# Gated outer-product attention and a leaky-ReLU MLP: from (chunk, batch) units to quads of four batches, with a new instruction order

## The chip, the cores and the metric

The kernel runs on one core of one Trainium2 chip. The metric is device time of one execution in microseconds (us), lower is better. The time before is 181.54 us, the median of three runs (181.17 to 182.75).

The engines of the core are named as in the profile: PE (matrix multiply, with PEld for its weight loads), ACT (scalar engine), DVE (vector engine), POOL (GpSimd) and SP, whose queue only issues DMAs here. Each engine works through its own list of instructions in order and waits at an instruction until what that instruction needs is there.

## The reference

There are 4 batches, 8 heads, 768 tokens, 48 elements per head. Per head a 48 x 48 state is decayed by a gate and gets an outer product at each token; the result y is laid out as 3072 tokens x 384 and goes through two matrix multiplies with a leaky ReLU between them.

```
f = 1.0 / (1.0 + np.exp(-f_logit))
for t in range(S):
    state = f[:, :, t, :, None] * state + np.einsum('bhd,bhe->bhde', k[:, :, t], v[:, :, t])
    y[:, :, t] = np.einsum('bhd,bhde->bhe', q[:, :, t], state)
...
h = x @ w_in                     # 3072 x 384  @  384 x 2048
g = np.maximum(0.01 * h, h)
return g @ w_out                 # 3072 x 2048 @ 2048 x 384
```

Inputs and output are float32; the matrix multiplies take bf16.

## The kernel before

**Tiling.** The sequence is cut into 6 chunks of 128 tokens. A unit `u` is one chunk of one batch, `u = 4 * chunk + batch`, so there are 24 units; a pair `m` is two neighbouring units. Inside a unit the recurrence is turned into matrix multiplies: cumulated log gates give two decay factors `em` and `a`; k is multiplied by `em` and q by `a`; both are turned so that the head's elements lie on the partitions; scores k x q are masked to the upper triangle; `mix` adds (state x q) and (scores x v); the state takes k x v and is scaled by the decay at the chunk's end (`a_end`).

**Chunk 0** (units 0 to 3) is already worked as one block of four batches, 4 neighbouring tokens per partition (functions with the prefix `q_`). The change leaves its arithmetic as it is.

**Chunks 1 to 5, before.** Each unit has tokens on the partitions. Its steps, with lines of the profile:

- `load_part` (L169): f, k, q and v of a unit, one DMA each on SP's queue, 128 tokens x 8 heads x 48 floats; each contiguous piece in memory is 48 floats, 192 bytes. There are 80 such loads.
- `gate_exp` (L339) and `gate_ln` (L342) on ACT; `gate_pe` (L348, L351): one 384-column matmul with the triangle `ut`, and four 1-column matmuls for the chunk's end; `decay_em` (L355), `decay_a` (L358, L360) on ACT, reading the matmul's bank.
- `k_scale` (L370) and `q_scale` (L374) on DVE or POOL; `cast_v` (L145).
- Turning k and q: by PE for units 4 to 9 (`turn_pe` L383, then `turn_k`, `turn_q`), by a DMA transpose for each pair from unit 10 on (`turn2_dma` L393).
- `score_pe` (L420; L428 for single units), `mask` (L431, DVE), `mix_pe` (L438 state part, L441 score part), `y_out`, `state_pe` (L449), `state_dve` (L457, L458), `state_pool` (L463, L332).
- Turning y: by PE (`x_pe` L472, `x_out`) for units 0 to 17, by DMA transposes (`x2_dma` L397) for pairs 9 to 11.
- `up` (L482): for one pair, a group `g` of two 128-wide slices of w_in, 3 matmuls of 256 columns each; `up_act` (L487, ACT) applies the leaky ReLU to a whole bank of 512 columns. Pair 2 goes as two single units (`up1`, L493, 128 columns).
- `down` (L502): a half is 8 matmuls of 384 columns for one unit; `put` copies the result out of PSUM and `out_dma` (L526) writes 128 rows. The last unit is cut into two column halves (`down_cols` L507, `put_cols`, `out_cols` L517).

**Order.** Nothing is scheduled by a compiler. After `manual_schedule()` a list of some 850 calls, written out one per line, gives the order of every engine's instructions and of SP's DMAs; the last argument of a call is the PSUM bank (0 to 7) that it uses. PE, ACT, DVE, POOL and SP each take their part of that list in that order. The weights come by DMAs on POOL's queue (`load_w_in` L185, two pieces; `load_w_out` L190, four pieces), placed in the list among chunk 0's steps. `idle_pe` (L137) puts matmuls on zeros into the early part.

## Time and profile before

| What | Value |
|---|---|
| time, median of 3 runs | 181.54 us (181.17 to 182.75) |
| profiled execution, span from first to last instruction | 180.2 us |
| granted PE clock | 0.998 |
| instructions | 4849 |
| DVE, ACT, POOL busy | 92.0, 124.4, 57.9 us |
| moved by DMA | 31.31 MB in 109398 packets, 100800 of them under 512 bytes |

The profile gives the span of the profiled execution and no time of its own beside it; the median of the runs is 1.3 us above the span, and that difference is what lies around the first and last instruction and between one execution and another. "Busy" for PE is from a matmul's start to its modelled end, and neighbouring matmuls overlap, so the time that a matmul costs is read from the distance between starts in the chain of waits, not from its own duration. The same holds for ACT and DVE, where an instruction begins before the one ahead of it has quite ended.

### The profile page before, as it was taken

To read this page: it belongs to the slowest core of one execution; us is meant where nothing else is said; L and a number is where in the kernel's file an instruction comes from. 1 tells how busy PE (TensorE), PEld (TensorE's weight loads), DVE (VectorE), ACT (ScalarE), POOL (GpSimd) and SP (SyncE) were. 2 spreads that over 40 slices of the span, in tenths; PEclk is the share of its full clock that TensorE was granted. 3 is DMA by queue.
4 is the path that set the end of the run, shared out by engine and by line. 5 is a ranking of instruction groups with operands and counts; after the bars stand their busy time and mean duration, and the time that the engine had idled before them with its cause. 6 is when DMAs were issued, how large, how long until landed. Compare 5 with 4: busy or idle time off the path is not lost.

```text
span 180.2 us, 4849 instructions
## 1 busy us (share of the span) xinstructions
PE 171.4 (95%) x1919; PEld 137.8 (76%) x1919; DVE 92.0 (51%) x211; ACT 124.4 (69%) x264; POOL 57.9 (32%) x107
## 2 busy tenths in 40 slices
PE   7689999999999999899999999999999999999992
PEld 5365899677878897597789687789876697798672
DVE  7779860287888735335376186696543266000000
ACT  2779999286887789767488776668795562596331
POOL 7077570023256444700446052634072100000000
PEclk9999999999999999999999999999999999999999
DMA  5999999899997989999699899999999982720112
GB/s 154 312 299 162 197 208 214 156 201 190 155 205 125 215 172 224 165 216 208 147 239 251 181 183 185 209 213 173 203 155 209 224 237 48 60 77 0 44 48 86
DMA packets 109398, 31.31 MB, mean 174 GB/s; under 512 B 100800, under 2 KB 108096, under 8 KB 109376
## 3 DMA queue, kind: packets, MB, share of 16 engines
q1 hardware_dynamic: 107440, 27.47, 79.5%
q0 software_dynamic: 1376, 3.15, 9.5%
q10 hardware_dynamic: 560, 0.39, 0.7%
q8 instruction: 15, 0.25, 0.7%
q14 instruction: 7, 0.06, 0.1%
HBM read 25.17 MB, written 4.72 MB: 166 GB/s over the span
## 4 chain that ended last, share of the span: by engine, by line
PE 58%; SPq 25%; DMA 11%; issue 1%; ACT 1%; DVE 1%; DVEq 0%
SPq L169 24%; PE ps L482 24%; PE ps L502 23%; DMA v_raw<-in_v_dram 6%; DMA f_raw<-in_f_logit_dram 3%; PE ps L420 2%; DMA fq<-in_f_logit_dram 2%; PE ps L441 2%; PE ps L507 1%; PE ps L438 1%; PE ps L348 1%; SPq L74 1%; PE ps L472 1%; PE ps L449 1%; DVE v_b L145 1%
## 5 line engine op out<-in xcount | busy, mean ns | idle before, releaser
L502 PE MATMUL ps<-w_out_b,gT 128*128 128x384 bf16 x368 | 65.9, 326 | 0.0
L487 ACT ACTIVATE gT<-ps 128x512 bf16<-128x512 f32 x88 | 51.5, 602 | 19.1 <-PE ps L482 16.7
L482 PE MATMUL ps<-xT,w_in 128*128 128x256 bf16 x528 | 63.3, 273 | 1.0 <-DVE xT L145 1.0
L482 PEld LDWEIGHTS <-w_in 128*128 128x128 bf16 x528 | 56.4, 114 | 3.0 <-issue 1.2
L502 PEld LDWEIGHTS <-gT 128*128 128x128 bf16 x368 | 34.6, 98 | 19.8
L431 DVE TENSOR_TENSOR wm<-ps,ut 128x512 bf16<-128x512 f32 x40 | 24.9, 683 | 14.5 <-ACT gT L487 4.9
L370 POOL TENSOR_TENSOR kqh<-k_raw,em_t 128x384 bf16<-128x384 f32 x12 | 11.4, 951 | 33.3 <-ACT em_t L355 28.1
L143 ACT COPY osb<-ps 128x384 f32<-128x384 f32 (+1 forms) x22 | 10.2, 465 | 17.0 <-PE ps L502 15.2
L332 POOL CAST sb<-sf 64x192 bf16<-64x192 f32 x40 | 14.5, 363 | 14.9 <-PE ps L438 12.8
L145 DVE CAST v_b<-v_raw 128x384 bf16<-128x384 f32 x14 | 7.1, 505 | 16.0 <-DMA v_raw<-in_v_dram 15.9
L374 DVE TENSOR_TENSOR kqh<-q_raw,a_t 128x384 bf16<-128x384 f32 x13 | 10.0, 770 | 8.0 <-DMA q_raw<-in_q_dram 7.3
L339 ACT ACTIVATE f_raw<-f_raw 128x384 f32<-128x384 f32 x20 | 10.6, 532 | 4.8 <-DMA f_raw<-in_f_logit_dram 4.6
L342 ACT ACTIVATE lf<-f_raw 128x384 bf16<-128x384 f32 x20 | 10.5, 527 | 0.4
L358 ACT ACTIVATE a_t<-ps 128x384 bf16<-128x384 f32 x20 | 9.8, 494 | 1.1 <-PE ps L351 0.9
L145 DVE CAST xn<-ps 128x384 bf16<-128x384 f32 x15 | 8.2, 556 | 4.1 <-PE ps L441 3.4
L355 ACT ACTIVATE em_t<-ps 128x384 bf16<-128x384 f32 x20 | 9.9, 501 | 0.2 <-PE ps L351 0.2
L463 POOL TENSOR_TENSOR sf<-sf,a_end 128x192 f32<-128x192 f32 x16 | 9.5, 592 | 0.4
L145 POOL CAST v_b<-v_raw 128x384 bf16<-128x384 f32 x6 | 3.1, 510 | 19.8 <-DMA v_raw<-in_v_dram 19.8
L137 PE MATMUL ps<-fill 128*128 128x256 bf16 x37 | 7.3, 353 | 1.4 <-DVE fill L102 1.3
L374 POOL TENSOR_TENSOR kqh<-q_raw,a_t 128x384 bf16<-128x384 f32 x7 | 7.0, 1003 | 4.2 <-issue 2.6
L370 DVE TENSOR_TENSOR kqh<-k_raw,em_t 128x384 bf16<-128x384 f32 x8 | 5.9, 752 | 3.7 <-ACT em_t L355 3.7
L441 PE MATMUL ps<-v_b,wm 128*128 128x48 bf16 x160 | 7.2, 183 | 0.0
(89 smaller groups left out, 201.8 us busy)
## 6 DMA issues: line engine op xcount, KB each, us to landing
out_dram<-osb SPq DMA_DIRECT2D x23, 192.0 KB, 3.4
f_raw<-in_f_logit_dram SPq DMA_DIRECT2D x20, 192.0 KB, 4.6
k_raw<-in_k_dram SPq DMA_DIRECT2D x20, 192.0 KB, 4.6
q_raw<-in_q_dram SPq DMA_DIRECT2D x20, 192.0 KB, 4.5
v_raw<-in_v_dram SPq DMA_DIRECT2D x20, 192.0 KB, 4.2
w_in<-in_moe_w_in_dram POOLq DMA_DIRECT2D x2, 768.0 KB, 9.8
w_out_b<-in_moe_w_out_dram POOLq DMA_DIRECT2D x4, 384.0 KB, 8.4
kq<-in_k_dram SPq DMA_DIRECT2D x1, 768.0 KB, 6.6
```

Source lines behind the costliest of these rows:

```text
L145: eng.tensor_copy(out=out, in_=in_)
L169: eng.dma_start(out=t, in_=src[b, :, c * C:(c + 1) * C, :].rearrange("h t d -> t h d"))
L332: nc.gpsimd.tensor_copy(out=state_b[b][r, :, e * D:(e + 1) * D], in_=state_f[b][r])
L339: nc.scalar.activation(raw[u]["f"], raw[u]["f"], AF.Exp, scale=-1.0)
L342: nc.scalar.activation(lfs[u % R_LF][:, :, 0:D], raw[u]["f"], AF.Ln, bias=1.0)
L370: eng.tensor_mul(khs[u % R_KQS][:, :, 0:D], raw[u]["k"], em_ts[u % R_EM])
L374: eng.tensor_mul(qhs[u % R_KQS][:, :, 0:D], r["q"], a_ts[u % R_EM])
L431: nc.vector.tensor_mul(wms[e][u % R_WM], bank(bk).rearrange("p (i n) -> p i n", i=P2), ut[:, None, :].to_broadcast([128, P2, 128]))
L441: nc.tensor.matmul(bank(bk)[:, h * D:(h + 1) * D], wms[h % 2][u % R_WM][:, h // 2, :], v_b[:, h, :], start=False, stop=(h == H - 1))
L482: nc.tensor.matmul(bank(bk)[:, i * 256:(i + 1) * 256].rearrange("p (a n) -> p a n", a=2), w_in_p[ff // 8][:, kk, ff // 4 % 2, :, ff % 4], ...
L487: nc.scalar.activation(gTs[m % GBUFS][:, 2 * g:2 * g + 2].rearrange("p f a n -> p (f a n)"), bank(bk), AF.Prelu, alpha=0.01)
L502: nc.tensor.matmul(bank(bk)[:, 0:KD], g_part(u)[:, ff, :], w_out_b[:, ff, :], start=(ff == 0), stop=(ff == NF - 1))
```

## The change

From chunk 1 on the unit of work for gates, loads, turning and `up` is a quad: one chunk of all four batches, laid out as chunk 0 already is. Partition `4t + b` holds 4 neighbouring tokens `4t .. 4t+3` of batch `b`.

- **Loads.** One f, one k and one q load for a chunk (`load_all`, contiguous pieces of 768 bytes, 768 KB), with two buffers each. v goes in four loads of 32 partitions (`load_v`), still in pieces of 192 bytes.
- **Gates.** ACT takes exp and ln on half the heads at a time, 128 x 768. Three additions on DVE or POOL (`g_sum`) cumulate within a partition, `g_cast` makes bf16 of the last, one 384-column matmul (`g_pe`) with a new matrix `before` sums over the partitions ahead of the same batch, four 4-column matmuls with `same` give the chunk's end, and `g_add` (DVE, 128 x 768, reading PSUM) adds that to all four tokens. `g_em` and `g_a` are the exponentials.
- **Scaling.** `g_k` and `g_q` write `khQ` and `qhQ`, each in four parts by pairs of heads, two on DVE and two on POOL as a rule.
- **Turning.** Chunks 1 and 2 by PE (`t_pe`, four groups of 8 transposes, `t_out`), chunks 3 to 5 by four DMA transposes each (`t_dma`). A copy `kh_dma` (four DMAs from SBUF to SBUF for chunks 1 to 4) brings k back to one batch per tile for `state_pe`.
- **Scores and mix** read the turned tiles with a step of four bf16 elements (8 bytes), both as weights and as the moving operand; the mask `utp` has the tokens in the permuted order.
- **Up.** `up4`: for a chunk, one 128-wide slice of w_in, 3 matmuls of 512 columns; `up4_act` takes the bank. For chunk 0 `up` stays at 256 columns.
- **Turning y.** By PE for chunks 0 to 2, by two DMA transposes each for chunks 3 to 5.
- **Down** is cut in quarters of 4 matmuls. Output rows are permuted, so a chunk is written by DMAs of 32 partitions (`outs_dma`), four for each group of batches; the last chunk by 16 of them, after the last `put`s.
- The list of calls is a new one.

The chunk's recurrence steps (`score_pe`, `mask`, `mix_pe`, `state_pe`, `state_dve`, `state_pool`, `y_out`) stay one per unit.

```diff
-    R_RAW, R_KQS, R_LF, R_EM, R_AEND, R_V, R_KQT, R_WM, R_XN, R_XT = 6, 4, 3, 3, 8, 6, 4, 4, 4, 4
+    R_WM, R_XN, R_XT = 4, 4, 2
...
-    def load_all(t, src):
+    def load_all(t, src, c=0):
         nc.sync.dma_start(out=t.rearrange("p h j d -> p h (j d)"),
-                          in_=src[:, :, 0:C, :].rearrange("b h (t j) d -> t b h (j d)", j=4))
+                          in_=src[:, :, c * C:(c + 1) * C, :].rearrange("b h (t j) d -> t b h (j d)", j=4))
...
+    def order_pe(bk):
+        f = four.rearrange("q t b -> q (t b)")
+        nc.tensor.matmul(bank(bk)[:, 0:128], f, f, start=True, stop=True)
+    def order_out(bk):
+        nc.vector.tensor_mul(before, bank(bk)[:, 0:128], us)
+        nc.vector.tensor_copy(out=same, in_=bank(bk)[:, 0:B])
...
-    def load_part(u, name, src, eng=nc.sync):
-        c, b = units[u]
-        t = raws[f"{name}_raw"][u % R_RAW]
-        eng.dma_start(out=t, in_=src[b, :, c * C:(c + 1) * C, :].rearrange("h t d -> t h d"))
+    def load_v(c, j):
+        nc.sync.dma_start(out=v_raws[c % 2][32 * j:32 * j + 32].rearrange("p b h d -> p (b h) d"),
+                          in_=v[:, :, c * C:(c + 1) * C, :].rearrange("b h (t j) d -> j t b h d", j=4)[j])
...
+    def g_exp(c, hh):
+        t = fqs[c % 2][:, 4 * hh:4 * hh + 4]
+        nc.scalar.activation(t, t, AF.Exp, scale=-1.0)
+    def g_sum(eng, c, j):
+        t = fqs[c % 2]
+        eng.tensor_add(t[:, :, j, :], t[:, :, j, :], t[:, :, j - 1, :])
+    def g_pe(c, bk):
+        t = lfb[c % 2]
+        nc.tensor.matmul(bank(bk)[:, 0:H * D], before, t[:, :, 0:D], start=True, stop=True)
+        if c < NCH - 1:
+            for p in range(P2):
+                nc.tensor.matmul(bank(bk)[:, H * D + B * p:H * D + B * p + B], t[:, 2 * p:2 * p + 2, :], same,
+                                 start=True, stop=True)
+    def g_add(c, hh, bk):
+        t = fqs[c % 2][:, 4 * hh:4 * hh + 4]
+        x = bank(bk)[:, 4 * hh * D:4 * hh * D + 4 * D].rearrange("p (h d) -> p h d", h=4)
+        nc.vector.tensor_add(t, t, x[:, :, None, :].to_broadcast([128, 4, 4, D]))
+    def scaled(eng, out, raw, by, p):
+        h = slice(2 * p, 2 * p + 2)
+        eng.tensor_mul(out[:, 8 * p:8 * p + 8, 0:D].rearrange("p (j e) d -> p j e d", e=2),
+                       raw[:, h].rearrange("p e j d -> p j e d"), by[:, h].rearrange("p e j d -> p j e d"))
+    def kh_dma(c, j):
+        nc.sync.dma_start(out=khu[c % 2][32 * j:32 * j + 32].rearrange("p b (a e) d -> p b a (e d)", e=2),
+                          in_=khQ[c % 2].rearrange("p (a j e) d -> p a j (e d)", a=P2, j=4)[:, :, j])
+    def t_dma(c, which, hh):
+        src, dst = ((khQ, kTs), (qhQ, qTs))[which]
+        nc.sync.dma_start_transpose(out=dst[c % 2][:, 2 * hh:2 * hh + 2].rearrange("p a j n -> p (a j) n"),
+                                    in_=src[c % 2][:, 16 * hh:16 * hh + 16].rearrange("p g d -> p (g d)"))
+    def turned(t, u, p):
+        c, b = units[u]
+        return t[c % 2][:, p].rearrange("q j (t b) -> q b (j t)", b=B)[:, b]
...
+    def up4(c, ff, bk):
+        for kk in range(NK):
+            nc.tensor.matmul(bank(bk).rearrange("p (a n) -> p a n", a=B), w_in_p[ff // 8][:, kk, ff // 4 % 2, :, ff % 4],
+                             xQs[c % R_XT][:, :, kk, :], start=(kk == 0), stop=(kk == NK - 1))
...
-    def down(u, half, bk):
-        for ff in range(8 * half, 8 * half + 8):
+    def down(u, part, bk):
+        for ff in range(4 * part, 4 * part + 4):
...
+    def outs_dma(c, j, b0=0, b1=B, c0=0, c1=KD, eng=nc.sync):
+        eng.dma_start(out=rows[c, j, :, b0:b1, c0:c1], in_=osbs[c % 2][32 * j:32 * j + 32, b0:b1, c0:c1])
```

The new list, where chunk 1's gates and turning stand (calls in order, several to a line):

```
state_pe(3, 0); g_exp(1, 0); order_pe(6); up(0, 6, 7); load_w_out(1); g_exp(1, 1); ...
up_act(1, 0, 3); g_cast(V, 1); up(1, 2, 4); up_act(1, 1, 0); g_pe(1, 6); up_act(1, 2, 4); up(1, 3, 1); g_add(1, 0, 6); ...
g_k(V, 1, 0); g_k(G, 1, 1); up(1, 7, 3); g_em(1, 1); down(0, 0, 0); g_a(1, 1); g_k(V, 1, 2); g_k(G, 1, 3); t_pe(1, 0, 0, 4)
... down(1, 0, 1); ... t_pe(1, 0, 1, 6); ... g_q(V, 1, 0); g_q(G, 1, 1); down(2, 0, 5); kh_dma(1, 1); ...
down(3, 0, 4); t_out(A, 1, 0, 1, 6); g_q(V, 1, 3); kh_dma(1, 3); t_pe(1, 1, 0, 7); t_pe(1, 1, 1, 2); load_v(1, 1); ...
```

and its end:

```
down(22, 3, 4); down(23, 3, 7); put(A, 22, 4); outs_dma(5, 0, 2, 3); put(A, 23, 7); outs_dma(5, 1, 2, 3); outs_dma(5, 2, 2, 3)
outs_dma(5, 3, 2, 3); outs_dma(5, 0, 3, 4); outs_dma(5, 1, 3, 4); outs_dma(5, 2, 3, 4); outs_dma(5, 3, 3, 4)
```

1708 lines of the change are left out of this document (842 added, 866 removed).

## The prediction

> **What bounds the kernel now.** I read the engine shares first, then the span cut into stages at the first `up` and at the last matmul's end, then the chain of waits for the price of each kind of matmul.
>
> ```profile
> PE 171.4 (95%) x1919; PEld 137.8 (76%) x1919; DVE 92.0 (51%) x211; ACT 124.4 (69%) x264; POOL 57.9 (32%) x107
> ```
> ```profile
> 21.10:57.00 35.90, 35.90 (x438) 29.58 (x436) 22.11 (x48) 27.91 (x61) 12.83 (x24) 1.00 1.10 184
> 57.00:97.00 40.00, 38.56 (x460) 31.83 (x457) 20.70 (x43) 29.26 (x66) 17.10 (x33) 1.00 0.99 201
> 97.00:137.00 40.00, 39.96 (x428) 32.12 (x426) 24.58 (x46) 29.86 (x67) 15.90 (x28) 1.00 1.10 189
> 137.00:177.05 40.05, 40.03 (x374) 32.20 (x372) 7.21 (x12) 21.40 (x40) 0.91 (x1) 1.00 0.46 102
> ```
> The columns are length, then busy time of PE, PEld, DVE, ACT and POOL, the clock, the DMA share and GB/s. From 21.10 to 177.05 PE stands still for 0.00 + 1.44 + 0.04 + 0.02 = 1.5 us. So PE's own list is the bound, at full clock: only fewer or cheaper matmuls, those 1.5 us, or the two ends can be won, and any new wait of PE is paid in full. The page calls DMA as busy as PE, but it costs only what shows in the 1.5 us.
>
> ```profile
> 59.46 0.45 PE ps L383 x8
> ...
> 60.24 0.67 PE ps L493 x12
> ...
> 89.36 0.17 PE ps L472 x3
> 89.52 0.55 PE ps L420 x16
> ...
> 91.48 0.16 PE ps L348
> 91.65 0.08 PE ps L351 x4
> ...
> 156.12 8.52 PE ps L482 x78
> 164.63 1.30 PE ps L502 x8
> ```
> This is the chain: start, length, line and count, so length by count is what one matmul takes of PE's time: 0.109 us for 256 columns (L482), 0.163 for 384 (L502), 0.056 for 128 (L493).
>
> **PE's work, part by part.** A 512-column matmul is not in the trace; from 256 to 384 columns the price rises by 0.053, so I take 0.216.
> - `up`: before 528 x 0.109 + 96 x 0.056 = 63.0; after 96 x 0.109 + 240 x 0.216 = 62.3. Gain 0.7. The column count is the same, so the halved number of matmuls gives little.
> - Gates: before 20 x 0.16 + 16 x 0.08 = 4.5; after 5 x 0.16 + 4 x 0.08 = 1.1. Gain 3.4.
> - Turning k and q by PE: 48 transposes become 64, at 0.45 / 8 = 0.056: loss 0.9. Turning y: 54 become 36 at 0.057: gain 1.0.
> - `down`, `mix` and `state_pe` keep count and columns: 0. One `order_pe` and one `idle_pe` less cancel.
>
> Sum: 4.2 us less work. Without any wait the span would be 180.2 - 4.2 - 1.5 = 174.5.
>
> **Scores with a step of 8 bytes.** `turned` makes both operands step four elements. No moving operand with such a step is in the trace; for weights there is one.
>
> ```profile
> L482 PEld LDWEIGHTS <-w_in x528: 111/114/136, 21.1 to 171.4; 128*128 128x128 bf16 x176
> ```
> ```profile
> L502 PEld LDWEIGHTS <-gT 128*128 128x128 bf16 x368 | 34.6, 98 | 19.8
> ```
> w_in is read with that step and loads in 114 ns, gT without it in 98. Scores come every 0.55 / 16 = 0.034 us; L493 loads w_in's stepped weights every 0.056 and does not wait for them. So a score costs between 0.034 and 0.056: 160 x 0 to 160 x 0.022 = 0 to 3.5. I take 0.6, near the low end, since 16 ns on a load that mostly lies under other matmuls is the nearest row. [...] The 16 ns on L482's loads speak against a stride that is free everywhere.
>
> **Loads of chunk 1.** In the list before, PE's first work for chunk 1 needed one unit (192 KB each of f, k, q). Now it needs 768 KB each, queued on SP behind v of chunk 0, while the weights move.
>
> ```profile
> 4.57 1.81 SPq L74 DMA_DIRECT2D gT<-in_v_dram  x1
> ```
> ```profile
> gT<-in_v_dram SPq DMA_DIRECT2D x1, 768.0 KB, 9.3
> ```
> ```profile
> q0 software_dynamic: 1376, 3.15, 9.5%
> ```
> ```profile
> q1 hardware_dynamic: 2671, 2.02, 108.7%
> ```
> ```profile
> q0 software_dynamic: 538, 1.08, 94.8%
> q1 hardware_dynamic: 538, 0.10, 15.3%
> ```
> ```profile
> 24.22 1.08 POOL L190 DMA_DIRECT2D w_out_b<-in_moe_w_out_dram  x2
> ```
> ```profile
> w_out_b<-in_moe_w_out_dram POOLq DMA_DIRECT2D x4, 384.0 KB, 8.4
> ```
> v is issued at 4.57 and has landed at 13.9. The weights are 1376 packets of queue q0 in all (the page). From 6 to 12 us (the fourth fence) SP's queue q1 moves 2671 packets of 768 bytes alone, 445 a us. From 18 to 24 us (the fifth) the weights run too, and the two queues move one packet each in turn, 538 to 538, at 90 a us. The weights end near 24.8 + 8.4 = 33. So of the 3 x 1024 packets of f, k and q some 900 pass before the weights start near 14, then one for each of the weights' 1376, and the last 800 go in 1.8 us after them. A 768-byte packet also takes longer per turn (1.087 x 96 us / 2671 = 39 ns against 0.153 x 96 / 538 = 27), 86 turns for each of 16 engines: the weights end 1 us later, their second piece for `up` about 0.6, which is paid inside the wait for q. q's last packet goes near 34 + 1.8, so q is there near 37 (1 us to land is my estimate); k is there near 31 to 32.
>
> PE gets to the first transposes of q after the first `up` (20.9) and 16 `up` (10.5), the gate and chunk 0's rest (1.0), two transpose groups (0.9) and four `down` quarters (2.6): about 36. The scaled q comes 0.6 to 1 us after the load and PE's second group needs all four parts, near 39. Wait: 2.5, between 0.5 (if the weights leave gaps) and 3.5. Ahead of it k is in time. Later loads come two chunks ahead at four times the packet size; their price is 0, as are the v loads, under the masks and `down` of chunk 0.
>
> **Pairs on DVE and POOL.** `g_k(V)` and `g_k(G)` are released by the same `g_em`.
>
> ```profile
> 92.87 0.60 DVE L370 TENSOR_TENSOR kqh<-k_raw,em_t 128x384 bf16<-128x384 f32 x1 [0.50 <-ACT em_t L355]
> ...
> 98.21 1.05 DVE L374 TENSOR_TENSOR kqh<-q_raw,a_t 128x384 bf16<-128x384 f32 x1
> ```
> ```profile
> 97.93 0.92 POOL L370 TENSOR_TENSOR kqh<-k_raw,em_t 128x384 bf16<-128x384 f32 x1 [1.01 <-POOL sb L332]
> ```
> The columns are start and length. Alone DVE takes 0.60; beside POOL's it ends at 99.26, 0.41 after POOL's end at 98.85. So a pair takes between 1.0 and 1.4. [...]
>
> ```profile
> L431 DVE TENSOR_TENSOR wm<-ps,ut 128x512 bf16<-128x512 f32 x40 | 24.9, 683 | 14.5 <-ACT gT L487 4.9 <-PE ps L420 3.7 <-ACT osb L143 3.5
> ```
> ```profile
> L234 ACT ACTIVATE fq<-fq 128x768 f32<-128x768 f32 x2 | 1.7, 836 | 1.9 <-DMA fq<-in_f_logit_dram 1.9
> ```
> `g_add` at 768 columns of PSUM is 1.0 by 683 ns for 512; `g_em` is 0.84 or less. Scaled k is there 0.2 + 1.0 + 0.8 + 1.4 = 3.4 after `g_pe`, each further pair 1.0 to 1.4 later. In chunk 2 PE has six `up4` (3.9) and then four transpose groups nearly in a row (0.45 each), while the pairs come every 1.0 to 1.4: wait 1.0 (0 to 2). In chunk 1 this lies under the wait for q.
>
> **Transposes by DMA, chunks 3 to 5.**
>
> ```profile
> L393 SPq DMA_TRANSPOSE kqT<-kqh x7: 1888/3307/4323, 73.7 to 141.7; - x7
> ...
> DMA to landing us min/median/max: 4.3/5.0/6.3
> ```
> ```profile
> L397 SPq DMA_TRANSPOSE xT<-xn x3: 1211/1217/1907, 136.5 to 154.1; - x3
> ...
> DMA to landing us min/median/max: 2.8/4.1/4.1
> ```
> L393 turns 16 blocks, L397 six; `t_dma` has eight, so I take 3.8 to landing. The last pair is scaled 6.5 to 7.7 after `g_pe`, landing at 10.3 to 11.5. PE reaches the scores after 15 `up4` and one `down` in chunk 4 (10.6), 14 and two in chunk 5 (10.5), later in chunk 3 (11.9). Wait: 0 to 1 in chunks 4 and 5 each; I take 1.4 together. What queues behind a waiting score on PE is everything.
>
> **ACT, SP, the rest.** ACT loses 80 gate instructions of 384 columns for 40 of 768: shorter, and it stood free for a fifth or more of each stage above; 0. DVE gains three `g_sum`, a cast and two `g_add` per quad, some 4.3 us in 25 of PE's; its busy share above leaves room; 0, apart from the waits already priced. `kh_dma` is due only after masks and `mix`; 0.
>
> **The end.**
>
> ```profile
> 177.07 0.32 ACT L143 COPY osb<-ps 128x192 f32<-128x192 f32 x1 [0.80 <-PE ps L507]
> 177.42 0.33 SPq L517 DMA_DIRECT2D out_dram<-osb  x1
> ```
> ```profile
> L143 ACT COPY osb<-ps 128x384 f32<-128x384 f32 x20 | 9.6, 479 | 15.3 <-PE ps L502 15.2
> ```
> Before, one half-width copy and one DMA follow the last matmul. Now the last `put` is 0.48 wide (384 columns) and eight DMAs are issued after unit 22's `put`, which ends 0.15 before the last matmul: at 0.37 each the last is issued 2.45 after it instead of 0.37. That is 2.1 more; if a 32-row DMA issues faster, 1.0. I take 1.9.
>
> **Sum.** 174.5 + 0.6 + 2.5 + 1.0 + 1.4 + 1.9 = 181.9 span. The median of the runs stands 1.3 above the span, so 183.2. No change that this measurement can tell means within 1%, 179.7 to 183.4.
>
> **The rivals.**
> - Faster: the waits hide. For it, the DMA view from 24 to 34 us:
>
> ```profile
> q0 software_dynamic: 538, 1.46, 73.7%
> q1 hardware_dynamic: 2615, 0.49, 28.2%
> ```
> The weights take only 73.7% of that stretch, so there are gaps in which q could come early. [...] Waits 1.0, end 1.0, scores 0: 176.5, time 177.8.
> - Slower by stepped scores: the moving operand's step binds each score at 0.056 instead of 0.035 to 0.038, on PE itself, in all five quads. For it: the 16 ns of L482. Price 3.5 instead of 0.6: time 186.1. It decides alone from 0.63 us for 16 scores on: there the time passes 183.4.
> - Slower by late transposes: at 16 blocks' median, 5.0 to landing, chunks 3, 4 and 5 wait 0.8, 2.1 and 2.2 instead of 1.4 in all: time 186.9. Against it: with four times fewer load packets the queue is emptier than at L393's 3.3 us.
>
> **How the numbers follow.** My own case (183.2, from 181 to 185.5): 0.45, of which 0.26 lies within 1% and 0.19 above. Faster: 0.24, of which 0.02 is within. Stepped scores 0.13, late transposes 0.18, of which 0.01 and 0.02 are within. So faster 0.22, same 0.31, slower 0.47. The range 178.0 to 187.0 reaches into both sides and leaves out about 2 in 10.
>
> **What would show it.** PE's stages: matmuls at 0.216 for `up4`; 16 scores in 0.55 or more; PE standing still just ahead of the third and fourth transpose group of chunk 1, released by q's load; short waits in chunk 2 released by DVE or POOL, in chunks 4 and 5 ahead of the scores, released by transposes; 5 us from the last matmul to the end. If PE is idle for under 2 us after its first `up`, or q lands before 35, I am wrong on the fast side; if a wait of over 2 us stands ahead of any score, on the slow side.

## The result, and the profile after

| What | Before | After |
|---|---|---|
| time, median of 4 runs | 181.35 us (179.52 to 182.75) | 203.68 us (202.5 to 205.18) |
| ratio, 95% interval | | 1.127 (1.117 to 1.136) |
| profiled execution: time, span | span 180.2 us | 202.81 us, span 201.1 us |
| granted PE clock | 0.998 | 0.957 |

The changed kernel is 12.7% slower; the ratio is taken from the fast runs alone, so it is not the quotient of the two medians. The forecast was 183.2 us, within 178 to 187: 20 us too low, and the range does not hold the time.

The engine rows and the queue row of the page after:

```profile
PE 178.1 (89%) x1550; PEld 113.3 (56%) x1550; DVE 108.1 (54%) x219; ACT 117.7 (59%) x215; POOL 66.1 (33%) x116
...
q1 hardware_dynamic: 69904, 29.63, 73.1%
```

The queue row of the page before (queue, packets, MB, share of 16 engines' span):

```profile
q1 hardware_dynamic: 107440, 27.47, 79.5%
```

A third fewer packets, yet 0.731 x 201.1 = 147.0 us of DMA time of this queue on each of the 16 DMA engines against 0.795 x 180.2 = 143.3. The larger loads saved packets, and something else used the time up.

The stages of the kernel after, from the first `up` on (length, busy time of PE, PEld, DVE, ACT, POOL, clock, DMA share, GB/s):

```profile
21.00:57.00 36.00, 33.34 (x348) 25.78 (x349) 25.55 (x53) 24.14 (x44) 12.32 (x24) 1.00 1.09 200
57.00:97.00 40.00, 35.12 (x276) 21.13 (x275) 28.56 (x47) 25.79 (x45) 18.93 (x30) 0.87 1.05 219
97.00:140.00 43.00, 37.24 (x327) 22.28 (x326) 24.79 (x50) 23.96 (x47) 11.10 (x20) 0.96 1.02 178
140.00:195.00 55.00, 54.90 (x373) 32.07 (x370) 11.57 (x17) 28.44 (x53) 8.57 (x14) 1.00 0.33 70
```

PE now stands still for 2.66 + 4.88 + 5.76 + 0.10 = 13.4 us, against 1.5 before, and it runs at a lower clock in two stages. The DMA share is over 1.0 until 140 us and a third after. The waits themselves, from PE's timeline (start, length; in brackets the idle time ahead and what ended it):

```profile
22.23 1.50 PE L473 MATMUL ps<-xQ,w_in 128*128 128x256 bf16 x12 [1.51 <-DMA w_in<-in_moe_w_in_dram]
27.33 4.78 PE L473 MATMUL ps<-xQ,w_in 128*128 128x256 bf16 x42 [1.38 <-DMA w_in<-in_moe_w_in_dram]
65.81 0.61 PE L398 MATMUL ps<-ident,khQ 128*128 128x128 bf16 x4 [3.58 <-ACT em_t L361]
...
103.24 1.35 PE L418 MATMUL ps<-qTs,kTs 64*128 64x128 bf16 x20 [0.38 <-DMA qTs<-qhQ]
...
120.45 9.88 PE L483 MATMUL ps<-xQ,w_in 128*128 128x512 bf16 x45 [2.23 <-DMA xQ<-xn]
...
132.30 1.35 PE L418 MATMUL ps<-qTs,kTs 64*128 64x128 bf16 x20 [1.15 <-DMA qTs<-qhQ]
```

The weights are late at the start, chunk 2 has a hole of 3.58 us, and later the turned y and the turned q are late. Behind the hole of chunk 2 the granted clock drops (slices of 5 us, columns as above):

```profile
60.00:65.00 5.00, 2.24 (x11) 0.94 (x9) 1.28 (x3) 1.51 (x4) 1.23 (x3) 0.95 1.01 269
65.00:70.00 5.00, 2.88 (x23) 2.02 (x24) 5.00 (x6) 4.81 (x8) 3.90 (x4) 0.50 1.00 262
70.00:75.00 5.00, 5.00 (x23) 2.34 (x23) 1.76 (x3) 1.40 (x3) 0.00 (x0) 0.52 1.10 122
```

And PE's own work, from the chain of waits:

```profile
75.00 1.52 PE ps L418 x24
...
91.50 8.43 PE ps L483 x39
```

An `up4` matmul costs 8.43 / 39 = 0.216 us, as forecast; a score costs 1.52 / 24 = 0.063, above the upper bound given for it (0.056).

### The profile page after: what moved, and what is told of

It reads as the page before. It is cut to its first block, busy times and chain, and to the rows that moved or that the text cites. A ratio compares the mean times of both kernels' runs of the same rounds, so it can differ in the third digit from the quotient of the medians.

```text
span 201.1 us, 4100 instructions
## 1 busy us (share of the span) xinstructions
PE 178.1 (89%) x1550; PEld 113.3 (56%) x1550; DVE 108.1 (54%) x219; ACT 117.7 (59%) x215; POOL 66.1 (33%) x116
## 4 chain that ended last, share of the span: by engine, by line
PE 45%; DMA 24%; SPq 13%; issue 6%; DVE 4%; POOL 3%; ACT 2%; POOLq 1%; DVEq 0%; ACTq 0%
PE ps L491 19%; PE ps L483 17%; DMA w_in<-in_moe_w_in_dram 7%; SPq L167 6%; DMA kh<-khQ 5%; DMA qq<-in_q_dram 4%; SPq L386 3%; DMA xQ<-xn 3%; DMA v_raw<-in_v_dram 3%; SPq L73 3%; PE ps L473 2%; PE ps L418 2%; POOL khQ L373 2%; DMA qTs<-qhQ 2%; DVE khQ L373 1%
## 5 line engine op out<-in xcount | busy, mean ns | idle before, releaser
L483 PE MATMUL ps<-xQ,w_in 128*128 128x512 bf16 x240 | 57.0, 391 | 2.2 <-DMA xQ<-xn 2.2
L483 PEld LDWEIGHTS <-w_in 128*128 128x128 bf16 x240 | 27.2, 115 | 26.5 <-issue 4.7
L422 DVE TENSOR_TENSOR wm<-ps,utp 128x512 bf16<-128x512 f32 x40 | 24.7, 681 | 19.2 <-PE ps L418 14.1
L147 ACT COPY osb<-ps 128x384 f32<-128x384 f32 x21 | 10.0, 478 | 28.7 <-PE ps L491 28.3
L373 POOL TENSOR_TENSOR khQ<-kq,em_t 128x384 bf16<-128x384 f32 x9 | 11.2, 1247 | 21.7 <-issue 19.2
L147 ACT CAST xn<-ps 128x384 bf16<-128x384 f32 x21 | 9.8, 478 | 13.3 <-PE ps L432 12.9
L357 DVE TENSOR_TENSOR fq<-fq,ps 128x768 f32<-128x768 f32 x10 | 9.4, 952 | 13.0 <-PE ps L348 7.8
L473 PE MATMUL ps<-xQ,w_in 128*128 128x256 bf16 x96 | 11.2, 273 | 2.9 <-DMA w_in<-in_moe_w_in_dram 2.9
L418 PE MATMUL ps<-qTs,kTs 64*128 64x128 bf16 x160 | 11.8, 292 | 2.1 <-DMA qTs<-qhQ 2.0
L473 PEld LDWEIGHTS <-w_in 128*128 128x128 bf16 x96 | 10.2, 114 | 3.2 <-DMA w_in<-in_moe_w_in_dram 3.2
L373 DVE TENSOR_TENSOR qhQ<-qq,a_t 128x384 bf16<-128x384 f32 x12 | 11.2, 955 | 0.4 <-ACT a_t L365 0.4
```

The source lines that it names most:

```text
L147: eng.copy(out=out, in_=in_)
L357: nc.vector.tensor_add(t, t, x[:, :, None, :].to_broadcast([128, 4, 4, D]))
L373: eng.tensor_mul(out[:, 8 * p:8 * p + 8, 0:D].rearrange("p (j e) d -> p j e d", e=2), raw[:, h].rearrange("p e j d -> p j e d"), by[:, h]. ...
L418: nc.tensor.matmul(bank(bks[e])[:, p * 128:(p + 1) * 128], turned(kTs, u, p)[r], turned(qTs, u, p)[r], start=True, stop=True)
L422: nc.vector.tensor_mul(wms[e][u % R_WM], bank(bk).rearrange("p (i n) -> p i n", i=P2), utp[:, None, :].to_broadcast([128, P2, 128]))
L473: nc.tensor.matmul(bank(bk)[:, i * 256:(i + 1) * 256].rearrange("p (a n) -> p a n", a=2), w_in_p[ff // 8][:, kk, ff // 4 % 2, :, ff % 4], ...
```

## The experiments

Times are medians, ratios are to runs of the kernel before on the same chip (179.9 to 180.2 us), each with its 95% interval. A difference between two variants is taken from their ratios, times 180; since the changed kernel's ratio is itself known to about 1%, a difference under 2 us shows nothing. Some of the kernels leave work out or read operands in another order, as their texts say, and compute other numbers: they measure prices and are no candidates.

| Run | Result | Ratio | Against the changed kernel |
|---|---|---|---|
| casts_behind | 202.52 | 1.126 (1.118 to 1.133) | -0.2 |
| fill_stall | 202.72 | 1.128 (1.120 to 1.137) | +0.3 |
| moving_plain | 202.47 | 1.122 (1.112 to 1.132) | -0.9 |
| weights_plain | 201.65 | 1.119 (1.110 to 1.128) | -1.4 |
| no_loads | 197.28 | 1.096 (1.091 to 1.101) | -5.5 |
| no_kh | 194.26 | 1.080 (1.074 to 1.087) | -8.3 |
| v_whole | 196.07 | 1.090 (1.084 to 1.095) | -6.7 |
| x_act | 202.56 | 1.125 (1.119 to 1.131) | -0.4 |
| v_natural | 198.20 | 1.103 (1.092 to 1.113) | -4.3 |
| weights_first | 214.77 | 1.196 (1.188 to 1.205) | +12.5 |
| tail_unit | 203.98 | 1.136 (1.128 to 1.144) | +1.6 |
| start_gate | 200.66 | 1.110 (1.103 to 1.117) | -3.1 |
| kh_wide | 208.18 | 1.156 (1.152 to 1.160) | +5.2 |
| kh_wide_pe | 200.37 | 1.113 (1.107 to 1.118) | -2.6 |
| light | 190.65 | 1.062 (1.054 to 1.070) | -11.6 |
| light_v | 187.74 | 1.042 (1.038 to 1.045) | -15.3 |
| light_v_gate | 184.33 | 1.023 (1.019 to 1.027) | -18.7 |
| before_copies (kernel before) | 186.03 | 1.032 (1.024 to 1.041) | |

### Chunk 2's order, the clock and the scores

The first reading of the trace was a sum of places: chunk 2's hole and the half clock behind it (8 us), the scores (4 to 5), the start, the late transposes. The hole has a plain cause in the list: `cast_v(V, 8)` waits on DVE for v, and `g_add(2, 1)` stands behind it. DVE's row in the changed kernel:

```profile
63.72 0.36 DVE L149 CAST v_b<-v_raw 128x384 bf16<-128x384 f32 x1 [4.41 <-DMA v_raw<-in_v_dram]
```

Four runs took single places away.

```
-    cast_v(G, 9)
-    cast_v(V, 8)
...
     g_q(G, 2, 3)
+    cast_v(V, 8)
+    cast_v(G, 9)
```

> The four casts of chunk 2's v (units 8 to 11) stand behind the scaling of k and q in the list instead of ahead of it; nothing else differs from the changed kernel. Theory: chunk 2's stall comes from the cast of unit 8, which waits on DVE for the v load and holds g_add and g_k of chunk 2. Then the 3.58 us gap of PE at 62.2 falls to under 1.5 us, the granted clock between 60 and 75 us stays at 0.95 or more instead of 0.50, and the time falls by 6 to 8 us (196 to 198, ratio 1.08 to 1.095). Rival 1, the DMA engines are the bound: the v load lands as late as before, mix of chunk 2 waits for it instead, and the time falls by under 2 us. [...]

```
+    idle_pe(36, 4)
     t_pe(2, 0, 0, 4)
```

> 36 matmuls of 256 columns on zeros (3.9 us at 0.109 each) stand ahead of the first transposes of chunk 2, so PE is busy while the data of chunk 2 is late; the lateness itself stays. Theory: the half clock after 65 us comes from PE standing still. Then the granted clock stays near 1.0 from 65 to 75 us and the time falls by 3 to 5 us (199 to 201, ratio 1.10 to 1.11). Rival: the half clock has another cause (a limit on power, or the load before it). Then the clock is 0.5 again from 65 to 75 us and the time is the same within 1 us (ratio 1.12 to 1.13).

```
+    def block_of(t, u, p):
+        c, b = units[u]
+        return t[c % 2][:, p, b, :]
...
-                nc.tensor.matmul(bank(bks[e])[:, p * 128:(p + 1) * 128], turned(kTs, u, p)[r], turned(qTs, u, p)[r],
+                nc.tensor.matmul(bank(bks[e])[:, p * 128:(p + 1) * 128], turned(kTs, u, p)[r], block_of(qTs, u, p)[r],
```

> The scores read q, their moving operand, from 128 neighbouring columns of the turned tile instead of with a step of 8 bytes; k, their weights, keep the step. The columns are not those of the unit, so the scores are other numbers. Theory: the step of the moving operand makes a score cost 0.065 us instead of 0.034. Then 8 scores take 0.27 to 0.30 us in the chain instead of 0.57, and the time falls by 4 to 5 us (ratio near 1.10). Rival: the stepped weights are the cost. Then 8 scores stay at 0.5 us or more and the time is the same within 1 us.

`weights_plain` is the same with `block_of` for kTs and `turned` for qTs.

> The scores read k, their weights, from 128 neighbouring columns of the turned tile instead of with a step of 8 bytes; q, the moving operand, keeps the step. The columns are not those of the unit, so the scores are other numbers. Theory: the moving operand's step is the cost; a weight load gets shorter (116 ns to some 95) but 8 scores stay at 0.5 us or more and the time is the same within 1 us. Rival: the stepped weights are the cost; 8 scores take 0.27 to 0.30 us and the time falls by 4 to 5 us (ratio near 1.10). If neither alone moves it, both steps share one limit, and only both plain would.

Each edit did what it was meant to do where it was made, and none moved the total by more than these runs can tell. Take `casts_behind`: the hole is gone but for two waits of 0.79 us and one of 0.23, and PE reaches chunk 2's scores at 68.25 instead of 74.93. Its waits later:

```profile
75.52 0.33 PE L440 MATMUL ps<-v_b,kh 128*128 128x96 bf16 x4 [2.02 <-DMA kh<-khQ]
93.87 4.69 PE L483 MATMUL ps<-xQ,w_in 128*128 128x512 bf16 x21 [1.73 <-ACT gT L487]
...
103.38 0.88 PE L418 MATMUL ps<-qTs,kTs 64*128 64x128 bf16 x12 [2.55 <-DMA qTs<-qhQ]
```

And its SP queue (start, length):

```profile
65.44 5.74 SPq L386 DMA_DIRECT2D kh<-khQ  x4
71.23 3.65 SPq L167 DMA_DIRECT2D v_raw<-in_v_dram  x3
74.97 3.59 SPq L507 DMA_DIRECT2D out_dram<-osb  x4
78.65 0.65 SPq L73 DMA_DIRECT2D fq<-in_f_logit_dram  x1
```

PE was 6.7 us ahead, but SP issued the f load at 78.65, as in the changed kernel:

```profile
78.27 0.65 SPq L73 DMA_DIRECT2D fq<-in_f_logit_dram  x1
```

ACT then waits 6.03 us for that load, and the steps of ACT, DVE and POOL that need it stand ahead of chunk 3's scaling in the list. So the time won in chunk 2 came back as waits for copies, gates and transposes: all but the first four of chunk 3's scores start at 103.38 here and at 103.24 in the changed kernel. That is the size that the first rival named (under 2 us); that the DMA engines are the bound is its reading, which the next section tests.

On the scores the pair of runs is clear about the place. The chain with q plain, then with k plain:

```profile
72.93 0.84 PE ps L422 x24
```
```profile
71.64 1.48 PE ps L422 x24
```

0.84 / 24 = 0.035 us with a plain moving operand, 1.48 / 24 = 0.062 with plain weights. The moving operand's step costs 0.063 - 0.035 = 0.028 a score, 4.5 us of PE over 160 scores; the weights' step costs nothing that shows.

The clock: with PE kept busy through chunk 2's hole, `fill_stall` shows

```profile
60.00:65.00 5.00, 5.00 (x37) 3.59 (x36) 1.29 (x3) 1.77 (x4) 1.25 (x3) 1.00 1.04 238
65.00:70.00 5.00, 3.40 (x38) 2.58 (x37) 5.00 (x6) 4.99 (x8) 3.89 (x4) 1.00 1.06 298
70.00:75.00 5.00, 5.00 (x53) 3.17 (x51) 3.69 (x7) 3.26 (x5) 0.00 (x0) 1.00 1.20 134
```

so the half clock followed from PE standing still. Its expected gain of 3 to 5 us did not come: PE reaches chunk 2's scores at 72.30, 2.6 us ahead of the changed kernel, then waits 2.06 us for the turned q of chunk 3 and starts those scores at 103.19, where the changed kernel starts them at 103.24.

### The DMA work

```
-    kh_dma(2, 0)
...
-    kh_dma(4, 3)
```

> The copies of k from SBUF to SBUF are left out in chunks 2 to 4 (state_pe reads the k of chunks 0 and 1), 12 of the 16 DMAs, 6144 packets of 256 bytes. Theory (DMA engines and SP's queue are the bound between 38 and 135 us): the time falls by 4 to 7 us (ratio 1.09 to 1.105), more than the 1.0 us for which PE waits for the copies themselves. Rival (each wait costs what PE's rows show): the time falls by 1 us, ratio 1.12.

The copies cost 8.3 us, the largest single term, though PE's own waits for them in the changed kernel come to 1.0. The queue shows why. The page's row for `no_kh` is

```profile
q1 hardware_dynamic: 63568, 28.06, 68.6%
```

0.686 x 192.1 = 131.8 us of DMA time, 15 less than with them, and between 80 and 115 us PE is busy all the time, where the changed kernel waits for copies and turned q. From 97 to 140 us PE stands still for 0.75 us instead of 5.76, at a clock of 1.00 instead of 0.96. So the copies were paid for the most part by what came behind them.

```
-    load_all(fqs[1], f_logit, 3)
-    load_all(kqs[1], k, 3)
...
-    load_all(qqs[1], q, 5)
```

> The nine f, k and q loads of chunks 3 to 5 are left out (chunks 3 to 5 work on what chunks 1 and 2 left in the buffers); v, the copies of k, the transposes and the output stay. That takes 9 x 1024 packets of 768 bytes off SP's queue. Theory now: from some 38 to 135 us the DMA engines are busy all the time and SP's one queue works in order, so that each wait taken from PE by another order comes back as a wait for a later transfer; the runs before this one (three edits that took 4 to 5 us each from the place they touched, and nothing or 1 us from the total) speak for it. Then the waits for k's copies, for the turned q and for the turned y in chunks 3 and 4 go, and the time falls by 7 to 11 us (ratio 1.065 to 1.09). Rival: what is lost lies in PE's and DVE's order and the scores; then the gain is under 3 us (ratio over 1.11).

5.5 us, between the two theories; the wait for copies in chunk 4 did not go, it grew from 0.57 to 1.91 us. Nine full loads gave back less than twelve small copies.

```
-    load_v(1, 0)
+    load_all(v_raws[1].rearrange("p b h d -> p (b h d)").rearrange("p (h j d) -> p h j d", h=H, j=4), v, 1)
...
-    load_v(1, 1)
...
-    load_v(1, 2)
...
-    load_v(1, 3)
...
```

> v of chunks 1 to 5 comes as f, k and q do, one DMA of 128 partitions and pieces of 768 bytes for a chunk, instead of four DMAs of 32 partitions and pieces of 192; the tokens then do not lie where scores and state expect them. Theory (DMA): 20480 packets become 5120, v no longer lands 6 us after its issue in four steps, the stall of chunk 2 goes, and the time falls by 5 to 9 us (ratio 1.075 to 1.10). Rival: the time stays within 2 us, since the order of the list decides.

Chunk 2's hole shrank to 0.79 twice and the time fell by 6.7, as the theory had it. That changes both the size of the pieces and the number of partitions. The next run keeps the size of the pieces and changes the partitions, and with them the order in memory: a DMA now takes neighbouring tokens of one batch, not every fourth token of four batches.

```
-    def load_v(c, j):
-        nc.sync.dma_start(out=v_raws[c % 2][32 * j:32 * j + 32].rearrange("p b h d -> p (b h) d"),
-                          in_=v[:, :, c * C:(c + 1) * C, :].rearrange("b h (t j) d -> j t b h d", j=4)[j])
+    def load_v(c, b):
+        nc.sync.dma_start(out=v_raws[c % 2][:, b],
+                          in_=v[b, :, c * C:(c + 1) * C, :].rearrange("h t d -> t h d"))
```

> v of chunks 1 to 5 comes by one DMA for a batch to 128 partitions, as in the kernel before, instead of one DMA for four batches to 32 partitions; pieces of 192 bytes, 20 DMAs and bytes stay the same; the tokens then lie in another order than the scores and the state expect. Theory: a 192-byte piece costs more DMA time in the 32-partition form than in the 128-partition form, and that is one of the things that used up what the larger f, k and q pieces saved. Then v lands in 4 to 5 us instead of 6.3 and the time falls by 2 to 5 us (ratio 1.10 to 1.115). Rival: the number of 192-byte pieces alone counts (the run with 768-byte pieces of v gained 6.6 to 7.6 us by them); then the time is the same within 1 us.

4.3 us with the same pieces and bytes. v lands in 5.4 us instead of 6.3, and the queue's time falls from 147.0 to 0.708 x 194.6 = 137.8 us. This pair of runs does not part the number of partitions from the order in memory.

```
-        nc.sync.dma_start_transpose(out=xQs[c % R_XT][:, w:w + 2].rearrange("p a f n -> p (a f) n"),
+        (nc.scalar if 6 <= m <= 9 else nc.sync).dma_start_transpose(out=xQs[c % R_XT][:, w:w + 2].rearrange("p a f n -> p (a f) n"),
```

> The four transposes of y of chunks 3 and 4 are issued by ACT on its own queue, right behind the copies that they read, instead of by SP behind the loads. Theory A (the place in SP's queue makes them late): the landing falls from up to 9.1 us to 3 to 4, PE no longer waits for xQ (2.2 us in the trace), and the time falls by 2 to 3 us. Theory B (the DMA engines are full, whoever issues): the landing stays over 5 us and the time is the same within 1 us.

Theory B: issued by ACT, the transposes of y took 5.1 us to landing (median), PE waited 3.16 us for them instead of 2.23, and the time did not move. SP was relieved all the same: two of these transposes had taken it 4.02 and 3.62 us to issue.

Was the kernel before free of this limit? Twelve copies that nobody reads, added to it:

```
+    def more():
+        nc.sync.dma_start(out=more_dst, in_=fill[:, None, 0:128].to_broadcast([128, 4, 128]))
...
     load_part(9, "k", k)
+    more()
```

> The kernel before with twelve more DMAs from SBUF to SBUF on SP's queue, 128 KB in pieces of 256 bytes each (the size and form of the copies of k), one behind the k load of each of units 9 to 20; nothing reads what they write. Theory: the DMA engines were already full from 35 to 137 us in the kernel before and PE had just no wait for them, so 6144 more pieces of some 27 ns on 16 engines, 10 us of DMA time, come out as PE waits: 4 to 9 us more, ratio 1.02 to 1.05. Rival: PE was the only bound and the DMA share shown was no limit; then the time is the same within 1 us.

5.8 us slower. The page of that run has

```profile
q1 hardware_dynamic: 113776, 29.04, 81.4%
```

0.814 x 182.9 = 148.9 us of DMA time, 5.6 more than the 143.3 before, where 10 were expected; that this is close to the 5.8 is chance, for the interval of the time is 4.3 to 7.3 us. From 20 to 160 us PE stands still for 4.8 us in that run and 1.5 in the kernel before. So the kernel before already stood at both limits, PE and DMA work, and a transfer that no one waits for was paid by someone who waits for the next.

One thing stays open: whether a copy costs by the time of the DMA engines or by its place in SP's queue, which issues in order. In the changed kernel SP stood at the copies for 19.9 us, 16.1 of them at the first of chunk 1, with loads behind it (time, number of waits, longest):

```profile
SPq L386 <- DVE khQ L373: 19.9, 2, 16.1
```

`x_act`, which relieved SP and gained nothing, speaks against the time of issue alone; no run parts the two.

```
-        scaled(eng, khQ[c % 2], kqs[c % 2], em_t, p)
+        h = slice(2 * p, 2 * p + 2)
+        eng.tensor_mul(khQ[c % 2].rearrange("p (j g) d -> p j g d", j=4)[:, :, h, 0:D],
+                       kqs[c % 2][:, h].rearrange("p e j d -> p j e d"), em_t[:, h].rearrange("p e j d -> p j e d"))
...
+        nc.sync.dma_start(out=khu[c % 2][32 * j:32 * j + 32].rearrange("p b h d -> p b (h d)"),
+                          in_=khQ[c % 2][:, 8 * j:8 * j + 8].rearrange("p g d -> p (g d)"))
```

> The scaled k is laid out with the token in the partition ahead of the head pair, so that each copy of k moves pieces of 1024 bytes instead of 256: 2048 pieces instead of 8192, same bytes, same result. The transposes of k in chunks 3 to 5 then wait for all heads and go by four smaller DMAs for a chunk instead of two. Theory (DMA time goes by pieces more than by bytes): a copy lands in under 3.5 us instead of 4.1, half of the copies' price comes back, and the time falls by 3 to 5 us (ratio 1.10 to 1.11), less what the later transposes cost (0 to 2 us). Rival: the copy as such costs, through its place in the queue; then the time falls by under 1 us or rises.

Slower by 5.2 us, though a copy landed in 3.6 us instead of 4.1. The halves of k's transposes, four for a chunk, took SP

```profile
123.08 5.12 SPq L398 DMA_TRANSPOSE kTs<-khQ  x4
```

5.12 / 4 = 1.28 us of issue each, no less than one of twice the size (1.25). Behind that issue time q's transposes came late: PE waited 2.92 and 1.12 us for the turned q of chunk 4, where the changed kernel waits 0.43 and 1.15. So this run says nothing of the pieces. `kh_wide_pe` is the same for chunks 1 and 2 alone, whose k PE turns:

> As the run with wide copies, but only for chunks 1 and 2, whose k PE turns; the transposes of chunks 3 to 5 stay as in the changed kernel. Eight of the sixteen copies move pieces of 1024 bytes instead of 256. Theory (pieces are the cost): 3072 pieces fewer, some 3 us of DMA time on 16 engines, come back in chunk 2 and after: the time falls by 1.5 to 3 us (ratio 1.11 to 1.12). Rival: the copy as such or its place in the queue is the cost; then the time is the same within 1 us (ratio 1.125 to 1.13).

2.6 us less, in the theory's range, at the edge of what two such intervals tell apart (1.107 to 1.118 against 1.117 to 1.136).

### The start and the end

```
-    load_all(fqs[1], f_logit, 1)
...
-    load_all(kqs[1], k, 1)
...
-    load_all(qqs[1], q, 1)
...
     q_back_out(A, 1, 0)
+    load_all(fqs[1], f_logit, 1, A)
...
+    load_all(kqs[1], k, 1, A)
     g_exp(1, 0)
...
     up_act(0, 7, 3)
+    load_all(qqs[1], q, 1, A)
```

> The f, k and q loads of chunk 1 are issued by ACT at some 14, 20 and 24 us, behind the start of the weights, instead of by SP at 6 to 13 us. Theory: at the start the weights' queue waits for these loads; then w_in's pieces land as before the change or earlier, PE's waits of 1.5 and 1.4 us for w_in go, and the first matmul of the second piece comes 2 to 3 us earlier; on the other side k and q of chunk 1 come later, and the total stays within 2 us of the changed kernel, since what bounds the middle is the DMA work in all and not its start. Rival: the later start runs through to the end; then the time falls by 2.5 to 3.5 us.

Beside the weights f took 21.0 us to land, and ACT, which copies for all of chunk 0, stood 13.60 us at `g_exp` behind it. So this run says nothing of the weights' start. The next one moves that start in another way:

```
-    load_all(kqs[1], k, 1)
...
     touch('q')
+    nc.sync.dma_start(out=seen_too, in_=seen)
+    load_all(kqs[1], k, 1)
```

> SP waits for chunk 0's q before it issues the k and q loads of chunk 1 (by a DMA of 4 bytes a partition behind the same sign that releases the weights); the order is otherwise that of the changed kernel. Theory: the weights then start at some 12.5 us instead of 16.2 and PE's two waits for w_in (1.5 and 1.4 us) go, but the time falls by under 1 us, since the DMA work of the middle is the same and lies no earlier. Rival: the late start runs through to the end; then the time falls by 2.5 to 3 us, ratio 1.11.

The rival's size held: 3.1 us less, with one wait for w_in of 0.86 left in place of 1.51 and 1.38. But it is not PE's lead that runs through. At 30 us PE is 1.8 us ahead; then it waits 0.50 and 0.37 us for chunk 1's turning, and it is ready for chunk 2's transposes at 62.1 us, against 62.2 in the changed kernel. What lasts is the lead of the DMA work. In the changed kernel the engines run dry while SP stands at chunk 1's first copy:

```profile
35.00:40.00 5.00, 4.96 (x54) 3.74 (x52) 3.86 (x7) 4.83 (x8) 3.62 (x3) 1.00 0.40 80
```

The DMA share from 30 to 60 us is 1.13 in `start_gate` and 1.04 in the changed kernel, which is 2.7 us more of DMA time, and the hole ahead of chunk 2's transposes shrinks from 3.58 us to 0.21, with the order of the list as it was.

```
-    outs_dma(5, 0, 3, 4)
-    outs_dma(5, 1, 3, 4)
-    outs_dma(5, 2, 3, 4)
-    outs_dma(5, 3, 3, 4)
+    def out_unit(c, b):
+        nc.sync.dma_start(out=rows[c, :, :, b, :], in_=osbs[c % 2][:, b])
...
+    out_unit(5, 3)
```

> The last chunk's output leaves by four DMAs, one for a unit with 128 partitions, instead of sixteen of 32 partitions. Theory: the 6.0 us from the last matmul's end to the end of the span are eight issues in a row on SP behind the last two copies; with two, they fall to 3.5 to 4.2 us and the time falls by 2 us (ratio 1.115). This is PE's own tail, on which no DMA work of the middle bears, so the gain shows in full. Rival: the issue of one DMA with 128 rows in four groups takes as long as four; then under 0.7 us.

No gain: one slow thing took the place of another. In the changed kernel the issue on SP is the limit, as the prediction had it:

```profile
189.82 8.76 SPq L512 DMA_DIRECT2D out_dram<-osb  x16
```

The last of the sixteen is issued by 198.58, 3.5 us after the last matmul's end at 195.08; before it was 177.75, 0.7 us after. The difference, 2.8 us, is all that the end lost. In `tail_unit` the last issue ends 1.1 us after the last matmul, yet the span ends 7.6 us after it instead of 6.0: here the transfer itself is slow. The DMA view of 194 to 202 us in this run, in 40 slices:

```profile
DMA  2222210332112122222222222322222100000000
GB/s 92 108 108 92 100 69 31 54 31 15 8 23 54 54 84 84 100 108 100 92 100 108 100 92 100 115 92 92 108 108 77 54 8 0 0 0 0 0 0 0
```

While the DMAs of 192 KB leave, the share stands at 0.2 and the rate at 100 GB/s, no more than the 101 to 102 GB/s at which the DMAs of 48 KB leave in the changed kernel (191 to 193 and 197 to 199 us). What holds the rate there is not shown.

### All together

`light` is `casts_behind`, `no_kh` and `moving_plain` in one; `light_v` adds `v_natural`; `light_v_gate` adds `start_gate`.

> Three edits at once: the copies of k left out in chunks 2 to 4, chunk 2's casts of v behind the scaling, and q read by the scores without a step (the scores are then other numbers, and the state of chunks 3 to 5 too). Theory: each cost its place some 4 to 8 us, and the order's and the scores' shares came back as waits for the copies only because the DMA queue stood full. With the copies gone all three count: 203.7 - 8.3 (measured for the copies alone) - 6 (chunk 2) - 4.5 (160 scores by 0.028 us) = 185, 183 to 188, ratio 1.02 to 1.045. Rival: the next transfers (f, k, q, v loads) take the place of the copies as the bound, as they did for the two single edits; then the time stays at 191 or more, ratio 1.06 and up, and the trace shows PE waits for loads or turned tiles.

> The kernel of three edits (copies of k left out in chunks 2 to 4, casts of chunk 2 behind the scaling, scores without the step) with v to 128 partitions as well. Theory: the DMA work is what is left; with v's form too the PE waits between 60 and 140 fall from some 5 us to under 2, and the time from 190.65 to 185 to 188 (ratio 1.03 to 1.045). What then remains above the forecast is the start (1.5 us later first matmul, 1.2 of wait for w_in) and the end (5.7 us against 3.2). Rival: the waits left are latency of the chain load, gate, scaling, transpose, not DMA work; then the gain is under 1.5 us.

> The kernel with copies of k left out in chunks 2 to 4, chunk 2's casts behind the scaling, scores without the step and v to 128 partitions, and SP waiting for chunk 0's q before it issues k and q of chunk 1. Theory: the start counts in full here as it did alone (3.0 us): 187.74 - 3 = 185, 184 to 186, ratio 1.02 to 1.035; what is left above the forecast is then the end (2.5 us later than before, 1.9 forecast) and some 1 us of small waits. Rival: with lighter DMA work the later loads have room and the start is absorbed; then the time is the same within 1 us.

`light`, at 190.65 and a ratio of 1.062, came out at the rival's bound: order and scores, worth nothing beside the copies, are worth 3.2 us without them and not the 10 that their places add up to; PE waits 2.00 us for the turned q of chunk 3 in that run. `light_v` came to the time that theory gave, with more waits left between 60 and 140 us than the 2 us it named (3.8 by the stages). `light_v_gate` came out as theory said. In `light_v_gate` PE's waits from 45 us on are these alone, and the clock is 1.00 in every stage:

```profile
62.14 0.40 PE L399 MATMUL ps<-ident,qhQ 128*128 128x128 bf16 x4 [0.79 <-DVE qhQ L374]
63.32 0.62 PE L399 MATMUL ps<-ident,khQ 128*128 128x128 bf16 x8 [0.79 <-DVE khQ L374]
65.27 1.46 PE L488 MATMUL ps<-xQ,w_in 128*128 128x512 bf16 x6 [0.23 <-DVE qTs L149]
93.82 0.75 PE L423 MATMUL ps<-qTs,kTs 64*128 64x128 bf16 x20 [0.22 <-DMA qTs<-qhQ]
116.57 0.31 PE L423 MATMUL ps<-qTs,kTs 64*128 64x128 bf16 x4 [0.20 <-ACT gT L492]
117.65 0.75 PE L423 MATMUL ps<-qTs,kTs 64*128 64x128 bf16 x20 [0.77 <-DMA qTs<-qhQ]
142.49 0.75 PE L423 MATMUL ps<-qTs,kTs 64*128 64x128 bf16 x20 [0.17 <-DMA qTs<-qhQ]
```

So the way from the changed kernel down is, in units of the time before: 1.127; without the copies 1.080; with order and scores 1.062; with v's form 1.042; with the start 1.023. Even this kernel, which leaves out twelve of the sixteen copies and reads q and v in another order than the result needs, is slower than the one before, so no version that beats both was in sight.

## Why the prediction was wrong

**The step that failed: "The page calls DMA as busy as PE, but it costs only what shows in the 1.5 us."** The DMA share of 1.0 to 1.1 in the stages was there to see, and it was read as work that PE hides. `before_copies` shows that it was a second limit: twelve copies that nobody reads made the kernel 5.8 us slower. From that premise came three prices of zero.

- **"`kh_dma` is due only after masks and `mix`; 0."** It measured 8.3 us. The step asked when the copies are needed and not what they take from the loads and transposes behind them, in engine time or in SP's queue.
- **"Later loads ... their price is 0, as are the v loads."** v's form (32 partitions, every fourth token) measured 4.3 us alone. The saving by larger pieces was real (for v 6.7 us in `v_whole`, against 4.3 by the form alone), but copies and v's form used it up: 147.0 us of DMA time against 143.3.
- **"ACT, SP, the rest ... DVE ... 0."** Busy share was weighed, and order was not. DVE and POOL meet casts that wait for a load ahead of scaling that does not; chunk 2's hole of 3.58 us and the half clock, which the prediction never mentions, came from that order and a late v together. Its price by itself is open: taken away alone it gave nothing, since the copies and the turned q were late next.

The two spans differ by 201.1 - 180.2 = 20.9 us. PE's waits are 13.4 - 1.5 = 11.9 of it, the scores 4.5, the end 2.8, and the lower clock some 5 (an estimate: PE's busy time in the slices from 60 to 75 and from 130 to 140 us, times the share of the clock withheld there, 0.05, 0.50, 0.48, 0.22 and 0.12). Less the 4.2 of work that was forecast as saved, that makes 20. The forecast had 3.4 of waits added, 0.6, 1.9 and no term for the clock.

**Stepped scores: right mechanism, wrong size.** 0.6 us was taken, 3.5 was the upper bound, 4.5 us of PE time measured. The bound came from L493, whose weights are stepped; the step that costs is that of the moving operand, which no row showed: 0.062 us a score with it, 0.035 without. The rival of stepped scores (186.1) had the right place and too low a bound.

**Loads of chunk 1: the wrong one was late.** q landed at 37.3, as forecast (near 37), and PE never waited for it. It waited 1.51 and 1.38 us for w_in, of which the step had only 0.6, "paid inside the wait for q", and so came to q's transposes at 39.2 instead of 36. 2.5 us were forecast for this wait; the 3.1 us that `start_gate` gained came by another way, so that the two sizes are close is luck. The 1 us to land in the forecast for q was the author's estimate; in the kernel before, v of chunk 0 landed at 13.9, 0.6 to 0.9 us after its last packet of 768 bytes.

**Pairs on DVE and POOL: within the range.** 1.0 (0 to 2) forecast in chunk 2; once the DMA work is light it is 0.79 + 0.79 = 1.6.

**Transposes by DMA: right for a queue that is not full.** 1.4 us (0 to 2) forecast for chunks 4 and 5; 0.77 + 0.17 = 0.9 in `light_v_gate`. In the changed kernel itself, chunk 4 alone waited 0.43 + 1.15, and chunk 3, which was given no wait, 0.38.

**PE's work: right but for the scores.** 0.216 us a matmul of 512 columns was forecast and measured.

**The end: right mechanism, too low.** 1.0 to 2.1 forecast, 1.9 taken. The last matmul starts its group at 184.52 and ends at 195.08, 6.0 us before the end of the span; before it was 177.03 and 3.2. That is 2.8 us more. The cause was given as eight issues on SP, at 0.37 each; the trace of the changed kernel bears that out, but they took 3.56 us, 0.44 each, and the last one ended 2.8 us later behind the last matmul than before. `tail_unit`, with two issues, was no faster because its transfers were slower.

**The rivals.** The fast one (177.8) took gaps in the DMA work for room in which q could come early; q landed at 37.3. Late transposes (186.9) named one symptom of the full queue, and priced it for three chunks as if nothing else were late with it. The sign set for the slow side, a wait of over 2 us ahead of a score, did not appear: the longest is 1.15 us. The long waits stood ahead of chunk 2's transposes (3.58), where 1.0 was taken, and of `up4` (2.23), which the prediction did not name.

The run without most of these troubles, `light_v_gate`, came to 184.33, near the 183.2 of the forecast. In part that is luck: it waits 0.37 us for q and has no stepped scores, for which the forecast took 3.1 together, and its ratio of 1.023 stands against 183.2 / 181.54 = 1.009. What held is the price of PE's work and the size of the short waits; the resource that the change leaned on was missing from the sum.

## What to carry to other kernels

When the DMA share stands near 1 through the stages that PE fills, DMA work can be a second bound, as it was here (a share of 1.0 to 1.1 before; twelve copies that nobody read cost 5.8 us): price every transfer added, moved or reshaped by its DMA time, whoever waits for it. Count the partitions and the order in memory as well as the size of the pieces (4.3 us for v), ask what stands behind each transfer in its queue, and look at what stands behind each waiting instruction on its engine. A wait seen in the trace is worth its length only if nothing else is late next (the hole of 3.58 us: 0.2 when it was taken away alone); take the suspects away together as well as one by one.

## What was not expected of the hardware

- The step of 8 bytes costs the moving operand 0.028 us on a score (64 x 128 by 128 columns) and the weights nothing that shows (0.063 us with both steps, 0.062 with plain weights).
- 192 KB loads into 32 partitions, of every fourth token, and into 128, of neighbouring tokens, in the same pieces of 192 bytes, differ by 9 us of DMA time in the whole queue over 20 loads (147.0 against 137.8).
- Issuing a DMA transpose takes SP 1.28 us for 4 blocks and 1.25 for 8.
- One hole of 3.58 us brought the clock to 0.50 to 0.52 over the next 10 us. Behind one of 2.55 us in `casts_behind` the clock was 0.68 from 105 to 110 us, and behind one of 2.02 us in the same run it stayed at 1.00.
- Output DMAs of 128 partitions (192 KB) left at 100 GB/s, no faster than those of 32 partitions (48 KB, 101 to 102 GB/s).
- The issue of one and the same copy of k took SP 0.64 to 1.03 us in the changed kernel; in `casts_behind` the four of chunk 2 took 5.74 us, 1.44 each.
